# H3 mixer and token MLP on one core: half of W1's first block loaded early, and x normed behind the last evacuations

## The chip, the core and the metric

The kernel runs on one core of a Trainium2 chip. The metric is the device time of one execution in microseconds; the median of three runs of the kernel before is 181.79 us (181.39 to 182.12). A profiled execution gives the trace that the prediction reads.

## The reference

All arrays are bfloat16, S = 2048 positions by D = 448 channels, F = 1792 hidden units. The first half is an H3 mixer: a four-tap shift convolution of k, a product with v, a causal long convolution over S by FFT, a gate with the normed x. The second half is an MLP over the token axis.

```
k_shift = sum_t k[s - 3 + t] * shift_k[:, 3 - t]
kv = k_shift * v
y  = irfft(rfft(kv padded to 2S) * rfft(ssm_k padded to 2S))[:S] + kv * ssm_D
h  = x + layernorm(x) * y                       # x = A_q
n  = layernorm(layernorm(h))
u  = gelu(einsum("sd,sf->df", n, w1) + b1)      # contraction over the S tokens
h2 = h + (einsum("df,fs->ds", u, w2) + b2).T
```

## The kernel before

The 2048 positions are held as 128 partitions by R = 16 rows, so that an activation is 16 tiles of 128 x 448. One large SBUF array ("arena") holds everything; its regions are reused by offset. TensorE writes into PSUM ("ps"), which has 8 banks of 128 x 448 f32.

The stages, in the order in which they are written:

- loads: SP issues the loads of k (KH), v (V), the filter (KN) and small vectors (L866 to L886).
- kv: TensorE transposes k (L936, reads KH), convolves with diagonal matrices (L955), DVE multiplies with v (L961).
- kT, k1, k2 and u1, u2: the FFT of the filter and of kv in two matmul stages (L1015, L1050), with evacuations on ACT or DVE (L717 to L721, L1025) and a shuffle across partitions by DMA between the stages (L1031, on POOL's and SP's queues).
- i1: DVE forms the complex products (L1083), TensorE the first inverse stage (L1095), the results are evacuated into TU (L717, L720), and DMAs shuffle them into TZ: L1119 for the first seven pairs of rows, L1108 for the last pair, split over the queues of POOL, SP and ACT.
- q and xn: statistics of x by row (bn_stats L1155, bn_aggr L1157, then POOL L1160 and L1163 for the reciprocal root); for the first NX = 4 rows x is also normed into XN (L1185 on ACT or L1187 on DVE), which lies over TK.
- warm: filler matmuls (L1129) while the last shuffle is under way.
- i2: for each row r two matmuls (L1215) read TZ row r, a gate on ACT or DVE (L1224, L1226) and a combination on DVE (L1234, or L1244 for the first four rows) make h in f32; sums and squares (L1262, or L1250 for rows 0 and 1), a short chain on POOL (L1272 to L1286) and a DVE normalization (L1293) make Q row r, the MLP's input.
- mlp: the first seven 128-wide chunks of F accumulate row by row in seven PSUM banks (L1340, weights W1A); the other seven run chunk by chunk (L1350, weights W1B), each with a gelu (L1330); then the second layer by output row (L1362, weights W2), a final add on DVE (L1365) and stores.

The weights come by emit_w1_load and emit_w2_load on SP: four loads for W1A (L1313), four for W1B (L1317), four for W2 (L1324). W1A row group h occupies the arena from byte 7168 h per partition; KH is bytes 0 to 14335, KT 17024 to 31359, so that the first two groups lie over KH and the other two over KT. All of them depend on shuf["zpool"], the last large shuffle DMA.

The instruction order is made by a small list planner in the file (class _Sched). Each step of a stage, a step being a new pair of stage name and time mark, takes its due time from the table WHEN, in the order in which the steps are emitted. Among the operations whose predecessors are done in the planner's model, each engine takes the one with the lowest due time. An operation that may run on ACT or DVE (FX) takes a letter from WHERE: a for ACT, d for DVE, f for either. A semaphore wait is emitted only for real dependencies (`preds`); the `safter` edges order the plan and nothing else.

Of the kernel before, what the change touches and what calls it, by code (L numbers as in the profile page):

```python
# [9 lines left out]

ENGS = ("pe", "act", "dve", "pool", "sp")
WHEN = {
    "dummy": (69,),
    "tables": (172, 222, 238, 115, 211, 90, 258, 324,),
    "loads": (189, 214, 205, 290, 237, 82, 264, 277, 251, 276, 104, 283, 244, 317, 322,),
    "kv": (253, 110, 128, 123, 135, 121, 85, 66, 113, 159, 149, 191, 230, 266, 235, 142, 275,),
    "kT": (114, 112, 155, 152, 96, 80, 177, 176,),
    "k1": (188, 194, 229, 249, 190, 192, 213, 216, 218, 221, 227, 241, 185, 255, 269, 284,),
    "k2": (93, 139, 239, 168, 180, 225, 273, 295, 321, 320, 313, 314, 262, 293, 318, 315,),
    "u1": (250, 270, 274, 304, 287, 299, 311, 316, 268, 271, 296, 298, 301, 303, 306, 307,),  # L20
    "xload": (291, 182, 300, 223,),
    "ct": (100,),
    "bias": (178,),
    "q": (248, 233, 76, 233, 234, 329, 330, 332, 333,),
    "u2": (89, 97, 118, 141, 132, 137, 117, 91, 199, 164, 246, 219, 145, 156, 278, 281,),
    "i1": (151, 43, 55, 45, 52, 46, 58, 51, 74, 67, 64, 61, 150, 88, 56, 54,),
    "xn": (215, 265, 285, 232, 207, 256,),
    "w1a": (208, 148, 107, 323,),
    "w1b": (130,),
    "warm": (184, 183, 158, 65, 62, 83, 57, 125, 126, 127, 63, 59, 86, 209, 210, 187, 179, 106, 129, 167, 161, 157,  # L30
        153, 206, 193, 181, 196, 120, 101, 72, 32, 0, 47, 169,),
    "i2": (170, 1, 327, 10, 15, 6, 138, 4, 49, 9, 14, 3, 7, 243, 11, 2, 13, 17, 242, 25, 108, 103, 111, 282, 40, 163,
        220, 197, 12, 31, 257, 247, 286, 35, 60, 99, 312, 160, 140, 254, 308, 44, 41, 68, 22, 20, 98, 133, 245, 261,
        38, 29, 204, 289, 162, 18, 26, 240, 305, 294, 202, 154, 102, 263, 259, 201, 309, 39, 302, 328, 16, 147, 71,
        200, 326, 325, 27, 42, 30, 174, 94, 297, 75, 267, 195, 203, 331, 36, 272, 186, 260, 136, 92, 165, 24, 116,
        292, 217, 53, 231, 95, 70, 124, 105, 23, 48,),
    "w2": (198,),
    "mlp": (280, 166, 171, 212, 50, 28, 134, 122, 119, 226, 37, 112, 81, 21, 19, 5, 87, 144, 34, 84, 33, 131, 79, 8,
        146, 78, 77, 175, 224, 310, 109, 236, 228, 279, 143, 173, 252, 73, 288, 319,),
}  # L40
WHERE = {
    "kv": "affdfaaf",
# [5 lines left out]
    "bias": "d",  # L48
    "u2": "dfaafdaafaffafaa",
    "i1": "aaaafaaaaaafdaff",  # L50
    "xn": "afdf",
    "i2": "fffadaaaaffd",
}


# [515 lines left out]
def _build(nc, A_q, A_k, A_v, A_shift_k, A_ssm_k, A_ssm_D, B_w1, B_b1, B_w2, B_b2, out):  # L571
# [5 lines left out]
    Bsz, S, D = A_q.shape  # L577
# [22 lines left out]
    o_TK = 31360  # L600
# [25 lines left out]
    with ctx:  # L626
        sch = _Sched(nc, ctx, n_dma_sems=112, small_off=SMALL)
# [26 lines left out]
        TU = view(o_TU, [R, 2, D])  # L654
# [40 lines left out]
        def Ppair(b):  # L695
            s0, s1 = b.slots
            return PS[:, s0:s1 + 1, 0:D]
# [342 lines left out]
        shuf = {}  # L1040
# [28 lines left out]
                     est={"act": 904.0, "dve": 600.0})  # L1069

        i1_last = []

        def emit_products_i1():
            for jj in range(R // 2):
                ms = []
                for h in range(2):
                    i = 2 * jj + h
                    sch.t0 = T_I1 + T_DI1 * i
                    m = _Buf(mring)
                    ms.append(m)  # L1080
                    ru = (o_TU + i * 2 * DB, 2 * DB)
                    aft = [x for w in wbufs for x in w.readers] if i == 0 else [mfirst[0]]
                    op("dve", lambda e, W, m=m, i=i: e.tensor_tensor(  # L1083
                        out=MR(m.slots[0]).rearrange("p (x y) d -> p x y d", x=2),
                        in0=TU[:, i].unsqueeze(2).broadcast_to([128, 2, 2, D]),
                        in1=TK[:, i].unsqueeze(1).broadcast_to([128, 2, 2, D]), op=ALU.mult),
                       r=[ru, (o_TK + i * 2 * DB, 2 * DB)], bw=[m], n=4 * D, after=aft)
                    if i == 0:
                        mfirst.append(len(sch.ops) - 1)
                bs = [_Buf(psum, 2) for _ in range(2)]  # L1090
                for h in range(2):
                    for t, (tab, xy) in enumerate(((MA, 0), (MN, 3), (MB, 1), (MB, 2))):
                        for par in range(2):
                            P = slice(64 * par, 64 * par + 64)
                            k = op("pe", lambda e, W, b=bs[h], m=ms[h], par=par, t=t, tab=tab, xy=xy, P=P: e.matmul(  # L1095
                                Pb(b, par), tab[P, :], MR(m.slots[0])[P, xy, :], start=(t == 0), stop=(t == 3)),
                               r=r_iv, br=[ms[h]], bw=[bs[h]], n=D, est=94.5, mode=3)
                            i1_last.append(k)
                    evac(lambda jj=jj, h=h: TU[:, 2 * jj:2 * jj + 2, h, :], lambda b=bs[h]: Ppair(b),
                         [(o_TU + (4 * jj + h) * DB, DB), (o_TU + (4 * jj + 2 + h) * DB, DB)], bs[h], 2 * D)  # L1100
                if jj == R // 2 - 1:
                    for h in range(2):
                        for par in range(2):
                            j = 2 * jj + par
                            p0 = 64 * (j & 1) + 32 * ((j >> 1) & 1) + (j >> 2)
                            o_h = o_TU + (2 * j + h) * DB
                            for q_, a, b_, j0 in (("sp" if h and par else "pool", 0, 112, 0), ("act" if h else "sp", 112, 128, 14)):
                                k = op(q_, lambda e, W, j=j, h=h, p0=p0, a=a, b_=b_, j0=j0: e.dma_start(  # L1108
                                    TZ[p0:p0 + 29:4, j0:j0 + (b_ - a) // 8, h, :], TU[a:b_, j, h, :]),
                                       r=[(o_h, DB)], w=[(o_TZ + j0 * 2 * DB, (b_ - a) // 8 * 2 * DB, "zpool" if a == 0 else "zsp")],  # L1110
                                       dmab=(b_ - a) * DB, keng=8)
                                if a == 0:
                                    shuf["zpool"] = k
                    continue
                for par in range(2):
                    j = 2 * jj + par
                    p0 = 64 * (j & 1) + 32 * ((j >> 1) & 1) + (j >> 2)
                    for q_, a, b_, j0 in (("pool", 0, 112, 0), ("sp", 112, 128, 14)):
                        shuf["z" + q_ + str(j)] = shuf["z" + q_] = op(q_, lambda e, W, j=j, p0=p0, a=a, b_=b_, j0=j0: e.dma_start(  # L1119
                            TZ[p0:p0 + 29:4, j0:j0 + (b_ - a) // 8].rearrange("p r c d -> p r (c d)"),  # L1120
                            TU[a:b_, j].rearrange("p c d -> p (c d)")),
                           r=[(o_TU + j * 2 * DB, 2 * DB)], w=[(o_TZ + j0 * 2 * DB, (b_ - a) // 8 * 2 * DB, "z" + q_)],
                           dmab=(b_ - a) * 2 * DB, keng=8)
# [43 lines left out]
        def emit_xn():  # L1167
            for g in range(NX // 2):
# [5 lines left out]
                   est=290.0, r=rs, w=[(x, 4) for x, _ in rw])  # L1174
# [4 lines left out]
                for i in range(2):  # L1179
                    r = 2 * g + i  # L1180
                    sch.t0 = T_Q + 0.5 + T_DQ * g + 0.1 * (i + 1)

                    def norm(e, W, r=r):
                        if W == "act":
                            return e.activation(out=XN[:, r, :], in_=X[:, r, :], func=ACT.Identity, bias=qx[:, r, 1:2],  # L1185
                                                scale=qs[:, r, 3:4])
                        return e.tensor_scalar(out=XN[:, r, :], in0=X[:, r, :], scalar1=qs[:, r, 0:1],  # L1187
                                               scalar2=qs[:, r, 3:4], op0=ALU.subtract, op1=ALU.mult)
                    op(FX, norm, r=[(o_X + r * DB, DB), (o_qst + 16 * r, 16), (o_qx + 8 * r, 8)],
                       w=[(o_TK + r * 4 * D, 4 * D)], n=D, est={"act": 590.0, "dve": 430.0})  # L1190

        GR = ((0, 1), (1, 1)) + tuple((2 + 2 * g, 2) for g in range(7))
        o_hst = small(10 * 64)
# [114 lines left out]
        def emit_w1_load(which):  # L1308
            for h in range(4):
                sch.t0 = (T_W1 - 30.0 * (h > 1), T_WB - 30.0)[which] + 0.1 * h * (1 - which)  # L1310
                rs = slice(4 * h, 4 * h + 4)
                if which == 0:
                    wl[0] = op(WQ, lambda e, W, rs=rs: e.dma_start(W1A[:, rs, :], w1d[:, rs, 0:896]),  # L1313
                       w=[(o_W1A + 4 * h * 1792, 4 * 1792)], dmab=128 * 4 * 1792,
                       after=[shuf["zpool"]], safter=(wl[0],) if h else ())
                else:
                    wl[0] = op(WQ, lambda e, W, rs=rs: e.dma_start(W1B[:, rs, :], w1d[:, rs, 896:1792]),  # L1317
                       w=[(o_W1B + 4 * h * 1792, 4 * 1792)], dmab=128 * 4 * 1792, after=[shuf["zpool"]], safter=(wl[0],))
# [106 lines left out]
```

## Time and profile before

| | us |
|---|---|
| median of three runs | 181.79 |
| profiled execution | 182.27 |
| its span, first to last instruction | 180.20 |
| PE busy | 170.7 |
| DVE busy | 104.8 |
| ACT busy | 91.2 |
| POOL busy | 63.2 |

The granted TensorE clock was 1.00 throughout. Busy time of PE is no measure of need, since filler matmuls count in it; the stages have different limits, so the profile is read by stage. A group's line gives the number of instructions, the busy time, and the idle time ahead of them with what ended it. The chain of waits follows the work that ended last back to the start.

### The profile page before, as it was taken

How to read it: one execution, taken by the hardware profiler on the slowest of the kernel's cores; microseconds unless marked ns; L12 is line 12 of the kernel's file. 1: busy time of each engine (PE TensorE's matmuls, PEld its weight loads, DVE VectorE, ACT ScalarE, POOL GpSimd, SP SyncE). 2: the span in 40 equal slices, each digit the busy share in tenths (PEclk: the TensorE clock that was granted, in tenths of full speed). 3: DMA queues.
4: the chain of work that ended last, by engine and by line, in shares of the span. 5: the costliest groups of instructions: out<-in, count | busy, mean ns of one | idle time of the engine just before them, and what ended most of it. 6: DMA issues, size and time to landing. Idle time of an engine off the chain costs nothing.

```text
span 180.2 us, 3395 instructions
## 1 busy us (share of the span) xinstructions
PE 170.7 (95%) x1333; PEld 97.5 (54%) x1333; DVE 104.8 (58%) x182; ACT 91.2 (51%) x129; POOL 63.2 (35%) x157
## 2 busy tenths in 40 slices
PE   6999999999889999898898999999999999999994
PEld 2888746543223332244343545556565677777784
DVE  7998677669889999999998645000000053322331
ACT  3897375689899999953985264710221100000000
POOL 8641209562950148797389953000000000000000
DMA  5997008686784947663999999990000001111122
GB/s 178 389 409 251 5 4 308 225 312 186 262 266 131 365 126 210 201 206 89 375 378 401 405 417 421 417 415 28 4 0 0 0 0 40 66 51 51 51 76 76
DMA packets 15347, 35.11 MB, mean 195 GB/s; under 512 B 3724, under 2 KB 9388, under 8 KB 15332
## 3 DMA queue, kind: packets, MB, share of 16 engines
q1 hardware_dynamic: 12068, 28.00, 41.8%
q0 software_dynamic: 3072, 6.80, 11.9%
q8 instruction: 10, 0.16, 0.4%
q10 hardware_dynamic: 192, 0.11, 0.2%
q14 instruction: 5, 0.04, 0.1%
HBM read 22.05 MB, written 1.84 MB: 133 GB/s over the span
## 4 chain that ended last, share of the span: by engine, by line
PE 65%; DVE 12%; ACT 10%; DMA 5%; POOL 3%; issue 2%; SPq 1%; DVEq 0%; POOLq 0%
PE ps L1362 23%; PE ps L1350 12%; PE ps L1340 9%; PE ps L955 7%; DVE arena L1083 5%; DMA arena<-arena 5%; PE ps L1015 4%; ACT arena L1025 4%; ACT arena L717 2%; PE ps L994 2%; PE ps L1050 2%; ACT arena L718 2%; PE ps L1095 1%; POOL arena L1286 1%; ACT arena L826 1%
## 5 line engine op out<-in xcount | busy, mean ns | idle before, releaser
L1362 PE MATMUL ps<-arena 128*128 128x448 bf16 (+2 forms) x238 | 43.5, 342 | 0.0
L1365 DVE SCALAR_TENSOR_TENSOR arena<-ps,arena 128x448 bf16<-128x448 f32 (+2 forms) x17 | 11.1, 656 | 54.2 <-PE ps L1362 54.2
L1362 PEld LDWEIGHTS ps<-arena 128*128 128x128 bf16 x238 | 32.9, 145 | 10.1 <-ACT arena L1330 0.8
L1340 PE MATMUL ps<-arena 128*128 128x448 bf16 x112 | 23.4, 353 | 0.6 <-DVE arena L1293 0.6
L1031 POOL DMA_DIRECT2D arena<-arena x32 | 17.5, 553 | 17.3 <-ACT arena L1025 16.3
L717 ACT CAST arena<-ps 128x896 bf16<-128x896 f32 x28 | 23.3, 979 | 0.4
L1350 PE MATMUL ps<-arena 128*128 128x448 bf16 x112 | 22.8, 352 | 0.0
L1025 ACT CAST arena<-ps 128x896 bf16<-128x896 f32 x22 | 18.9, 913 | 6.6 <-PE ps L1015 5.7
L1330 ACT ACTIVATE arena<-ps,arena 128x448 bf16<-128x448 f32 x14 | 8.3, 638 | 22.4 <-PE ps L1350 18.7
L1050 PE MATMUL ps<-arena 128*64 128x448 bf16 x128 | 16.0, 361 | 1.1 <-ACT arena L1025 0.7
L1340 PEld LDWEIGHTS ps<-arena 128*128 128x128 bf16 x112 | 10.6, 98 | 11.5 <-DVE arena L1293 2.2
L1083 DVE TENSOR_TENSOR arena<-arena 128x1792 bf16<-128x1792 bf16 x16 | 16.6, 1083 | 0.1
L1350 PEld LDWEIGHTS ps<-arena 128*128 128x128 bf16 x112 | 10.9, 98 | 10.1 <-DVE arena L1226 0.3
L1095 PE MATMUL ps<-arena 64*128 64x448 bf16 x128 | 14.1, 351 | 1.7 <-ACT arena L717 1.0
L1015 PE MATMUL ps<-arena 128*32 128x448 bf16 x256 | 14.8, 355 | 0.5 <-ACT arena L718 0.3
L955 PE MATMUL ps<-arena 112*128 112x224 bf16 (+3 forms) x112 | 13.4, 273 | 0.0
L1119 POOL DMA_DIRECT2D arena<-arena x14 | 8.3, 595 | 12.7 <-ACT arena L717 12.3
L955 PEld LDWEIGHTS ps<-arena 112*128 112x128 bf16 x112 | 9.2, 98 | 4.4 <-DVE arena L1025 0.9
L1050 PEld LDWEIGHTS ps<-arena 128*64 128x64 f16 x128 | 5.3, 108 | 11.4 <-ACT arena L717 3.7
L1262 ACT ACTIVATE arena<-arena 128x448 bf16<-128x448 f32 x14 | 8.1, 576 | 6.1 <-DVE arena L1234 6.0
L961 DVE TENSOR_TENSOR arena<-ps,arena 128x896 bf16<-128x896 f32 x8 | 8.6, 1089 | 4.3 <-PE ps L955 4.2
L1095 PEld LDWEIGHTS ps<-arena 64*128 64x128 f16 x128 | 5.0, 94 | 10.7 <-ACT arena L717 6.0
(93 smaller groups left out, 209.6 us busy)
## 6 DMA issues: line engine op xcount, KB each, us to landing
arena<-in_B_w_dram SPq DMA_DIRECT2D x8, 896.0 KB, 12.1
arena<-in_B_w_dram SPq DMA_DIRECT2D x2, 2048.0 KB, 17.0
arena<-arena SPq DMA_DIRECT2D x16, 224.0 KB, 3.2
arena<-arena POOLq DMA_DIRECT2D x32, 112.0 KB, 3.4
arena<-in_B_w_dram SPq DMA_DIRECT2D x2, 1536.0 KB, 19.5
arena<-arena POOLq DMA_DIRECT2D x14, 196.0 KB, 4.2
arena<-in_A_k_dram SPq DMA_DIRECT2D x4, 448.0 KB, 6.0
arena<-in_A_v_dram SPq DMA_DIRECT2D x4, 448.0 KB, 9.9
```

Of the source, the lines that this page charges most:

```text
L717: return e.copy(out=dst(), in_=src())
L955: op("pe", lambda e, W, b=b, i=i, cc=cc, dl=dl, i0=i0, i1=i1, rs=rs, sh=sh: e.matmul(Pb(b, i)[:, 112 * i0:112 * i1 + 112], KX[cc][0:112, i ...
L1015: op("pe", lambda e, W, b=b, r=r, q=q, x=x, c0=c0: e.matmul(PS[32 * q:32 * q + 32, b.slots[x], 0:D], E[:, 2 * r + x, c0:c0 + 32], src[:, r ...
L1025: return e.copy(out=dst, in_=Ppair(b)) if W == "act" else e.tensor_copy(out=dst, in_=Ppair(b))
L1031: shuf[tag].append(op(q_, lambda e, W, g=g, i=i, a=a, nu=nu, jh=jh: e.dma_start(T[a + i:a + i + 4 * nu - 3:4].rearrange("p (j k) c d -> p ...
L1050: op("pe", lambda e, W, b=bs[h], h=h, j=j, c=c, par=par: e.matmul(PS[64 * par:64 * par + 64, b.slots[c], 0:D], FW[:, 64 * c:64 * c + 64], ...
L1083: op("dve", lambda e, W, m=m, i=i: e.tensor_tensor(out=MR(m.slots[0]).rearrange("p (x y) d -> p x y d", x=2), in0=TU[:, i].unsqueeze(2).br ...
L1095: k = op("pe", lambda e, W, b=bs[h], m=ms[h], par=par, t=t, tab=tab, xy=xy, P=P: e.matmul(Pb(b, par), tab[P, :], MR(m.slots[0])[P, xy, :], ...
L1340: op("pe", lambda e, W, r=r, fc=fc, b=bs[fc]: e.matmul(Pb(b), W1A[:, r, 128 * fc:128 * fc + 128], Q[:, r, :], start=(r == 0), stop=(r == R ...
L1350: op("pe", lambda e, W, r=r, fc=fc, b=b: e.matmul(Pb(b), W1B[:, r, 128 * (fc - n0):128 * (fc - n0) + 128], Q[:, r, :], start=(r == 0), sto ...
L1362: op("pe", lambda e, W, r=r, fc=fc, b=b, d0=d0, d1=d1: e.matmul(Pb(b)[:, d0:d1], W2[fc // 7][:, fc % 7, r:S:R], G[:, fc, d0:d1], start=(fc ...
L1365: op("dve", lambda e, W, r=r, b=b, A=A, d0=d0, d1=d1: e.scalar_tensor_tensor(out=X[:, r, d0:d1], in0=Pb(b)[:, d0:d1], scalar=bm[:, r:r + 1 ...
```

## The change

Three edits are made.

1. In emit_w1_load the first two groups of W1A no longer depend on shuf["zpool"]; what is left is that KH must have been read. The other two keep the dependency.
2. The norms of x for the first four rows get a `safter` edge on the last evacuation of i1.
3. The due times in WHEN are given as decimals. Sorted by due time, all entries outside q, xn, warm, i2 and mlp stand in the same order as before; those five have other values. The letters of xn and i2 in WHERE change.

```diff
-    "w1a": (208, 148, 107, 323,),
+    "w1a": (2654.22, 2601.22, 2565.22, 2779.22,),
...
-    "q": (248, 233, 76, 233, 234, 329, 330, 332, 333,),
+    "q": (2686.67, 2692.38, 2558.85, 2728.33, 2726.2, 2724.82, 2729.2, 2733.43, 2725.05,),
...
-    "xn": (215, 265, 285, 232, 207, 256,),
+    "xn": (2725.33, 2727.89, 2403.48, 2719.09, 2605.55, 2614.65,),
...
-    "i2": (170, 1, 327, 10, 15, 6, 138, 4, 49, 9, 14, 3, 7, 243, 11, 2, 13, 17, 242, 25, 108, 103, 111, 282, 40, 163,
+    "i2": (2602.37, 0, 2723.32, 764.4, 756.9, 1409.88, 2536.4, 934.78, 1089.89, 765.9, 756.4, 1486.7, 1497, 2662.27,
...
-    "xn": "afdf",
-    "i2": "fffadaaaaffd",
+    "xn": "addf",
+    "i2": "aaffafaaddff",
...
         i1_last = []
+        evl = []
...
-                    evac(lambda jj=jj, h=h: TU[:, 2 * jj:2 * jj + 2, h, :], lambda b=bs[h]: Ppair(b),
+                    ke = evac(lambda jj=jj, h=h: TU[:, 2 * jj:2 * jj + 2, h, :], lambda b=bs[h]: Ppair(b),
                          [(o_TU + (4 * jj + h) * DB, DB), (o_TU + (4 * jj + 2 + h) * DB, DB)], bs[h], 2 * D)
                 if jj == R // 2 - 1:
+                    evl.append(ke)
...
                     op(FX, norm, r=[(o_X + r * DB, DB), (o_qst + 16 * r, 16), (o_qx + 8 * r, 8)],
-                       w=[(o_TK + r * 4 * D, 4 * D)], n=D, est={"act": 590.0, "dve": 430.0})
+                       w=[(o_TK + r * 4 * D, 4 * D)], n=D, est={"act": 590.0, "dve": 430.0}, safter=evl)
...
             for h in range(4):
                 sch.t0 = (T_W1 - 30.0 * (h > 1), T_WB - 30.0)[which] + 0.1 * h * (1 - which)
+                if which == 0 and h < 2:
+                    sch.t0 = -5.0 + h
                 rs = slice(4 * h, 4 * h + 4)
                 if which == 0:
                     wl[0] = op(WQ, lambda e, W, rs=rs: e.dma_start(W1A[:, rs, :], w1d[:, rs, 0:896]),
                        w=[(o_W1A + 4 * h * 1792, 4 * 1792)], dmab=128 * 4 * 1792,
-                       after=[shuf["zpool"]], safter=(wl[0],) if h else ())
+                       after=[shuf["zpool"]] if h > 1 else (), safter=(wl[0],) if h else ())
```

## The prediction, made before the change was run

> **What bounds the kernel now.** I read the chain of waits first, to see which stretches set the end, then busy time by stage, then each engine in order of time around the seam at 77 to 97 us. Of the chain:
>
> ```profile
> 78.28 0.67 SPq L1108
> ...
> 79.00 4.93 DMA arena<-arena
> ...
> 83.97 0.57 PE ps L1215 x2
> ...
> 96.10 0.57 DVE arena L1293
> ...
> 96.71 6.85 PE ps L1340 x35
> ...
> 141.84 35.47 PE ps L1362 x196
> ```
>
> The columns are start, length and what ran. A block transfer bridges 79.00 to 83.93; a chain of small work runs from there to 96.71; from 96.71 to 177.32 every piece is TensorE. The view by stage:
>
> ```profile
> 77.20:83.97 6.77, 6.22 (x32) 3.04 (x33) 6.38 (x22) 2.79 (x4) 6.15 (x14) 1.00 0.61 175
> 83.97:89.56 5.59, 4.91 (x25) 2.37 (x26) 5.24 (x16) 4.21 (x8) 1.87 (x5) 1.00 0.79 269
> 89.56:96.71 7.15, 6.57 (x34) 2.96 (x33) 6.09 (x19) 5.68 (x16) 6.57 (x15) 1.00 1.05 387
> 96.71:108.40 11.69, 11.69 (x62) 5.75 (x63) 7.82 (x23) 5.41 (x13) 8.64 (x21) 1.00 1.04 410
> ```
>
> Columns: window, length, busy us (instructions) of PE, weight loads, DVE, ACT, POOL, then clock, DMA share, GB/s. PE's 6.22 us in the first row is filler (L1129). From 96.71 on PE runs 62 matmuls in 11.69 us, 0.189 us each, without a hole. So the kernel is a front part up to 96.71, an 80.6 us PE block that only fewer matmuls would shorten, and a 2.9 us tail. The question is whether the change brings 96.71 forward.
>
> The timelines of the engines at the seam:
>
> ```profile
> 76.14 1.39 SPq L1119 DMA_DIRECT2D arena<-arena  x2
> 77.57 2.11 SPq L1108 DMA_DIRECT2D arena<-arena  x3
> ```
> ```profile
> 77.02 0.76 ACT L1185 ACTIVATE arena<-arena 128x448 f32<-128x448 bf16 x1
> 77.68 0.89 ACT L717 CAST arena<-ps 128x896 bf16<-128x896 f32 x1
> 78.61 1.98 ACTq L1108 DMA_DIRECT2D arena<-arena  x2
> ```
> ```profile
> 78.75 0.24 POOL L1160 TENSOR_SCALAR arena<-arena 128x2 f32<-128x2 f32 x1
> 79.06 0.63 POOL L1108 DMA_DIRECT2D arena<-arena  x1
> ```
>
> The reader sees a norm of x (L1185) in front of the last evacuation (L717), whose input, the last L1095 matmul, is done at 77.09. The reader should also see that SP issues without a break from 76.14 to 79.68.
>
> **What the skill says.** "DMA: Bandwidth & Descriptors", section "Issuing engines are not separate DMA queues": transfers of all issuing engines share the same 16 engines, so an early load is free only where these are idle. The trace agrees: they are 0.02 busy in 18 to 27 us (last fence below) and 1.04 busy in the third and fourth rows above. "Anatomy of one DMA" on the same page gives about 2 us fixed per transfer; the seam's 98 KB pieces take 4.3 to 5.0 us from issue to landing, so the trace's number is used. "Perfetto Trace Analysis", section "Identifying the Most-Contended Engine", warns that matmul busy time misleads; I count matmuls at 0.189 us instead.
>
> **Part 1, half of W1A early.** Rows 0 to 7 of W1A lie over KH, last read by the transposes L936 (last at 15.3 us). SP has nothing to issue between 9.4 and 26.40 us, so both loads go out at about 15.5, at 0.4 to 0.7 us each (L1313's issues). Nothing queues behind their wait but the first shuffles at 26.40.
>
> ```profile
> 18.00:27.00 9.00, 8.98 (x118) 5.43 (x116) 6.08 (x9) 4.84 (x6) 1.56 (x4) 1.00 0.02 4
> ```
>
> They carry 2 x 917.5 KB; at the 410 GB/s of the fourth row above that is 4.5 us, behind the input loads that drain at about 18. Landing: about 23, 3 us before the first shuffle. Cost 0; upper bound 0.5 us if late inputs (the small bias loads, on which L914 waits until 19.8) are disturbed. POOL's queue issues nothing there until 26.69.
>
> At the other end L1313 issues two loads instead of four after 83.94, and everything behind moves 4.5 us forward. Does anyone wait for it? No wait at L1340 or L1350 names a weight DMA. The first L1340 (89.56) starts after Q of L1293 (88.82 + 0.48 = 89.30), while its weights landed at 83.94 + 4.7 = 88.6. W1B's last load lands at 93.7 + 13.2 = 106.9, before its first use at 108.36. All weight waits are covered before and better covered after. Value: 0 in the old order. It opens up to 0.7 us only if Q comes earlier than 88.6, the point from which W1A would be next in line.
>
> **Part 2, norms behind the last evacuation.** The extra edge orders the planner's list only; no semaphore is added. It takes L1185 (0.76 us) from in front of L717, which can then start at about 77.15 instead of 77.68: 0.53 us. Where does that go? POOL's last L1108 waits for this evacuation and could issue at 78.75 instead of 79.06: 0.3 us. But SP's third L1108 carries the other part of the same data, and SP is busy issuing until 78.95; the evacuation was over at 78.57 already. So SP's train is next in line, and nothing in the change shortens it. The reading L1215 needs every piece. Bounds 0 to 0.5 us of gain; I take 0.1.
>
> The norms themselves (ACT 0.76, DVE 0.56) move behind 77.2. Engines before: three on ACT, one on DVE; after, the letters "addf" put two on DVE, one on ACT, one free. ACT is idle from 82.17 to 85.32, so its share is hidden. DVE gains 0.5 us inside 77.20 to 83.97, where it is 6.38 of 6.77 busy with the statistics L1155 (12 rows by 84.2 at about 0.6 us with their L1157). So about one row of statistics slides behind 83.97.
>
> **Part 3, the order of the second half.** Sorted by due time, all entries outside q, xn, warm, i2 and mlp stand as before, so the plan up to about 67 us should be the old one. Those five are shuffled: agreement in rank between old and new i2 entries is only about 0.3. On PE the second-layer inputs I2 still begin with row 0; the front groups of rows 0 and 1 stay near the front on DVE; the six pairs of statistics after the first two stand together in the middle (places 255 to 272 of 335) where two were first and four last. Gates fixed to DVE change from rows 8 and 15 to 12 and 13.
>
> What can be won: in 83.97 to 96.71 (12.74 us) PE runs 26 L1215, 28 L1340 and 4 fillers, 58 x 0.189 = 10.9 us, so 1.8 us of holes and 0.75 of fillers: at most 2.5. What can be lost: DVE is idle 0.35 + 1.06 = 1.4 us in the same stretch; added work there beyond that delays Q. Added at most: the displaced row 0.6, the last pair of statistics that now runs at 97.78 (1.35 with its aggregates), and up to two more gates of 0.65 drawn in: 3.2, so a loss of at most 1.8. The old trace does not show the new order. Nothing in it says which way; I take 0, with -2.5 and +1.8 kept for the range.
>
> **Sum.** 0 + (-0.1) + 0 = -0.1 us. The profiled execution took 182.27 us with a span of 180.20, so 2.07 lie outside the span; it stands 0.48 above the median 181.79. The sum is a difference of spans: profiled 182.2, median 181.7.
>
> **The cases.** About 0.9 us (0.5%) is what a measurement here can tell from no change.
>
> 1. Forecast: L1215 starts within 0.3 us of 83.97 and the fill takes as long as before, 181.7; own range 180.9 to 182.6. For: SP's unbroken train, covered weights, a PE-bound block. Against: an entirely new order. Chance 0.43.
>
> 2. Faster: the new order, with W1A's first half resident, feeds PE without holes, so half of the 2.5 us goes: 181.7 - 1.2 = 180.5, at the utmost 179.2. For: L1340 waits 2.2 us on L1293 in this stretch, and L1215 1.1 us on ACT's gates; that is order, not work. Against: the rstd path POOL L1272 to L1286 (1.03 + 0.5 + 0.5 and more) stays. Chance 0.25.
>
> 3. Slower: DVE takes over in 83.97 to 96.71. Its 1.4 us of slack take the second norm and one displaced row of statistics (1.1); from there on the pair drawn from 97.78 and gates on DVE stand in front of Q. With 2.7 us added, L1293's Q are 1.3 late and so is PE's gapless block: 183.1, at the utmost 183.6. For: the norms go to DVE, statistics leave last place, DVE is 11.33 of 12.74 busy. Against: DVE has 3.9 us idle in the next window. Chance 0.28.
>
> 4. The change doesn't do what it says: the early loads are planned late or the free evacuation goes to DVE behind statistics, and all stays at 181.8. Chance 0.04.
>
> **Numbers.** Predicted 181.7. The range 180.3 to 183.2 takes in most of cases 2 and 3; the likeliest one's own range is 180.9 to 182.6. Faster by over 0.5% (below 180.9): case 2 but for a little, 0.25. Slower (above 182.7): case 3, 0.29 with the edge of case 1. Same: 0.46.
>
> **What would show it.** Right: two L1313 issues at 15 to 17 us and an idle DMA slice filled; first shuffle still at 26.4; last L717 ending near 78.05; SP's last L1108 still near 79.0 and the first L1215 near 83.9; PE gapless from 96 to 97. Case 2: gapless before 95.8. Case 3: after 97.6, with L1340 waiting for L1293 behind L1155 on DVE. I would be wrong in kind if the early loads push the first L1031, if SP's train begins earlier than 76.1, or if a hole opens in the block after 97.

## The result, and the profile after

The changed kernel takes 185.19 us (median of four runs, 184.48 to 185.5) where the kernel before took 181.95 beside it (four runs): ratio 1.0181, 95% interval 1.0162 to 1.02. It is slower by 3.2 us, outside the predicted range. Its profiled execution took 185.5 us with a span of 183.3, against 182.27 and 180.20.

In kernel.py of the changed kernel the lines lie 14 to 18 further down: the products with v are L975, the bias cast L928, the first shuffle L1045, the second inverse stage L1231, its gate L1240 (ACT) or L1242 (DVE), statistics of x L1171, L1173, L1176, L1179, sums of a pair on POOL L1288, L1291, L1293, L1298, the reciprocal root L1302, Q L1309, the first layer L1358 and L1368, the second L1380. I call the stretch that begins with the first L1215 (L1231) the fill: in it the 16 rows of Q are made and the first layer starts.

The chain of waits of the changed kernel, in order of time (start, length, what ran):

```profile
8.73 11.75 DMA arena<-in_B_b_dram
...
20.51 0.04 DVE arena L928
...
20.59 1.10 DVE arena L975
...
84.43 0.93 PE ps L1231 x4
...
89.25 0.98 POOL arena L1302
...
100.59 0.72 POOL arena L1179
...
101.30 0.66 POOL arena L1302
...
103.00 0.68 POOL arena L1179
...
103.70 0.70 DVE arena L1242
...
104.45 0.55 PE ps L1231 x2
...
144.02 36.42 PE ps L1380 x201
```

Two things are new in it. At the front stands the small load of b2 and the bias cast L928 behind it. And in the fill the chain stays on POOL from 89.25 until 103.68, goes by a gate on DVE, and gives way to TensorE only at 104.45; before it was TensorE's from 96.71 on.

The view by stage, same windows and columns as in the prediction:

```profile
77.20:83.97 6.77, 6.68 (x39) 3.18 (x35) 6.54 (x23) 2.82 (x4) 6.65 (x15) 1.00 0.64 179
83.97:89.56 5.59, 4.73 (x25) 2.17 (x23) 5.36 (x18) 3.39 (x7) 2.58 (x7) 1.00 0.74 243
89.56:96.71 7.15, 5.95 (x21) 2.40 (x22) 6.54 (x21) 6.23 (x17) 6.40 (x13) 0.76 1.05 399
96.71:108.40 11.69, 11.18 (x60) 5.43 (x58) 8.04 (x22) 4.42 (x12) 9.38 (x24) 1.00 1.03 417
```

In the third row PE ran 21 matmuls where it ran 34 before. The timelines of SP and of DVE (start, length, instruction, idle time ahead of it with its releaser):

```profile
15.61 0.95 SPq L1331 DMA_DIRECT2D arena<-in_B_w_dram  x2
27.12 26.69 SPq L1045 DMA_DIRECT2D arena<-arena  x16
...
78.07 2.19 SPq L1124 DMA_DIRECT2D arena<-arena  x3
```
```profile
20.51 0.17 DVE L928 CAST arena<-arena 128x16 f32<-128x16 bf16 x1 [2.15 <-DMA arena<-in_B_b_dram]
20.59 2.08 DVE L975 TENSOR_TENSOR arena<-ps,arena 128x896 bf16<-128x896 f32 x2
...
84.03 1.12 DVE L1171 BATCH_NORM_STATS2 arena<-arena 128x6 f32<-128x448 bf16 x2
85.38 1.28 DVE L1260 SCALAR_TENSOR_TENSOR arena<-ps,arena 128x448 f32<-128x448 f32 x2 [0.23 <-PE ps L1231]
```

The early loads are issued where the prediction had them, at 15.61. The first shuffle comes at 27.12 instead of 26.40, and the fill begins at 84.43 instead of 83.97. The span grew by 3.1 us: 0.46 of it lies ahead of the fill, and 2.64 from the fill's start to the end (183.3 - 84.43 = 98.87 against 180.20 - 83.97 = 96.23). Two statistics of x (L1171) run from 84.03 to 85.15, across the start of the fill; before, the last one there ended at 84.21, 0.24 us after its start:

```profile
83.62 0.59 DVE L1155 BATCH_NORM_STATS2 arena<-arena 128x6 f32<-128x448 bf16 x1
```

### The profile page after: what moved, and what is told of

Same layout as the page of the kernel before. It is cut to its first block, busy times and chain, and to the rows that moved or that the text cites. A ratio compares the mean times of both kernels' runs of the same rounds, so it can differ in the third digit from the quotient of the medians.

```text
span 183.3 us, 3392 instructions
## 1 busy us (share of the span) xinstructions
PE 172.9 (94%) x1333; PEld 98.2 (54%) x1333; DVE 105.3 (57%) x183; ACT 90.6 (49%) x128; POOL 62.9 (34%) x157
## 4 chain that ended last, share of the span: by engine, by line
PE 60%; ACT 13%; POOL 7%; DMA 6%; DVE 6%; SPq 4%; issue 2%; DVEq 0%; POOLq 0%
PE ps L1380 23%; PE ps L1368 12%; DMA arena<-in_B_b_dram 6%; PE ps L1358 6%; ACT arena L731 6%; PE ps L1029 5%; ACT arena L1039 5%; PE ps L969 5%; PE ps L1145 4%; ACT arena L732 3%; PE ps L1064 3%; PE ps L1110 2%; POOL arena L1302 2%; DVE arena L1098 2%; DVE arena L1260 1%
## 5 line engine op out<-in xcount | busy, mean ns | idle before, releaser
L1380 PE MATMUL ps<-arena 128*128 128x448 bf16 (+2 forms) x238 | 44.0, 342 | 0.0
L1380 PEld LDWEIGHTS ps<-arena 128*128 128x128 bf16 x238 | 32.7, 145 | 10.7 <-ACT arena L1348 1.9
L1358 PE MATMUL ps<-arena 128*128 128x448 bf16 x112 | 25.0, 367 | 0.7 <-DVE arena L1309 0.7
L1045 POOL DMA_DIRECT2D arena<-arena x32 | 17.5, 553 | 17.8 <-ACT arena L1039 16.8
L1368 PE MATMUL ps<-arena 128*128 128x448 bf16 x112 | 22.7, 352 | 0.0
L1348 ACT ACTIVATE arena<-ps,arena 128x448 bf16<-128x448 f32 x14 | 8.9, 633 | 24.5 <-PE ps L1368 19.8
L1358 PEld LDWEIGHTS ps<-arena 128*128 128x128 bf16 x112 | 11.2, 102 | 12.1 <-issue 1.8
L1368 PEld LDWEIGHTS ps<-arena 128*128 128x128 bf16 x112 | 10.9, 98 | 10.1 <-ACT arena L1348 0.7
L1064 PEld LDWEIGHTS ps<-arena 128*64 128x64 f16 x128 | 5.3, 108 | 11.3 <-ACT arena L731 3.7
L975 DVE TENSOR_TENSOR arena<-ps,arena 128x896 bf16<-128x896 f32 x8 | 8.6, 1090 | 4.3 <-PE ps L969 4.2
```

The lines of the kernel that those rows point to most:

```text
L1045: shuf[tag].append(op(q_, lambda e, W, g=g, i=i, a=a, nu=nu, jh=jh: e.dma_start(T[a + i:a + i + 4 * nu - 3:4].rearrange("p (j k) c d -> p ...
L1064: op("pe", lambda e, W, b=bs[h], h=h, j=j, c=c, par=par: e.matmul(PS[64 * par:64 * par + 64, b.slots[c], 0:D], FW[:, 64 * c:64 * c + 64], ...
L1358: op("pe", lambda e, W, r=r, fc=fc, b=bs[fc]: e.matmul(Pb(b), W1A[:, r, 128 * fc:128 * fc + 128], Q[:, r, :], start=(r == 0), stop=(r == R ...
L1368: op("pe", lambda e, W, r=r, fc=fc, b=b: e.matmul(Pb(b), W1B[:, r, 128 * (fc - n0):128 * (fc - n0) + 128], Q[:, r, :], start=(r == 0), sto ...
L1380: op("pe", lambda e, W, r=r, fc=fc, b=b, d0=d0, d1=d1: e.matmul(Pb(b)[:, d0:d1], W2[fc // 7][:, fc % 7, r:S:R], G[:, fc, d0:d1], start=(fc ...
```

## The experiments

Each kernel was timed beside the kernel before on the same chip, and the ratio is to that. In the first four the kernel before took 181.77 us. Diffs are cut to the lines that matter.

**Which of the three edits.** Four kernels take them apart: the early load alone; the changed kernel with its first half of W1A behind the shuffle again; early load and edge with the old table; the edge alone (its list of the last evacuations, evl, is filled as in the change).

```diff
  early load alone (on the kernel before)
-                       after=[shuf["zpool"]], safter=(wl[0],) if h else ())
+                       after=[shuf["zpool"]] if h > 1 else (), safter=(wl[0],) if h else ())
  new table without early load (on the changed kernel)
-                       after=[shuf["zpool"]] if h > 1 else (), safter=(wl[0],) if h else ())
+                       after=[shuf["zpool"]], safter=(wl[0],) if h else ())
  edge alone (on the kernel before)
-                       w=[(o_TK + r * 4 * D, 4 * D)], n=D, est={"act": 590.0, "dve": 430.0})
+                       w=[(o_TK + r * 4 * D, 4 * D)], n=D, est={"act": 590.0, "dve": 430.0}, safter=evl)
```

> The kernel before with the early load of two W1A groups alone; old due times, no edge. Theory A (two separate losses: the early load delays the small bias load, behind which DVE's multiplications with v queue, and the new order starves the fill): the bias cast starts 0.5 to 0.8 us later than before (20.3 to 20.6 us), the first L1215 is 0.4 to 0.5 later (84.4), time 182.3 to 182.6. Rival B (the early load carries the whole loss through the DMA queues): about 185. Rival C (the early load is free and the 0.7 us of the trace is scatter): 181.9, cast at 19.8.

> The changed kernel with all four W1A loads behind the last shuffle again; new due times and edge stay. Theory A: the front is back to the old times (first L1231 at 83.9 to 84.0), the fill is as starved as in the changed kernel, time 184.5 to 184.8. Rival B: 181.9. Rival C: 185.2.

> The changed kernel with the old due times and letters; early load and edge stay. Theory A: the early load's 0.4 to 0.5 us minus at most 0.3 from the edge: 182.0 to 182.5, and a gapless PE block from about 97. Rival B: about 185. Rival C: 181.6 to 181.9.

> The kernel before with the planner's edge alone. If SP's row of issues sets the last shuffle, as predicted, the last evacuation ends 0.5 us earlier, the first L1215 stays within 0.3 us of 83.97 and the time at 181.6 to 181.9. If the evacuation sets it, the first L1215 comes 0.5 us earlier and the time is 181.3 to 181.5.

| kernel | us | ratio, interval | cast starts | first shuffle | fill starts | span |
|---|---|---|---|---|---|---|
| before (profile) | | | 19.79 | 26.40 | 83.97 | 180.2 |
| early load alone | 182.45 | 1.0034 (1.0021 to 1.0048) | 21.09 | 27.70 | 84.59 | 181.0 |
| new table, no early load | 184.23 | 1.0142 (1.012 to 1.0163) | 19.66 | 26.27 | 83.25 | 182.0 |
| early load and edge, old table | 182.75 | 1.0063 (1.004 to 1.0087) | 20.36 | 26.97 | 84.41 | 180.6 |
| edge alone | 182.04 | 1.0014 (1.0004 to 1.0023) | 19.29 | 26.15 | 83.10 | 179.6 |
| changed kernel | 185.19 | 1.0181 (1.0162 to 1.02) | 20.51 | 27.12 | 84.43 | 183.3 |

The early load costs 0.34%, the edge gains nothing, and the new table carries 1.42%. Early load and new table make 1.76%, the changed kernel's 1.81% within the intervals. Under the new table the edge changes no instruction's place, so that the kernel without the early load is also the new table by itself. The times came within 0.3 us of what was expected for two separate losses. One expectation failed in kind: if SP's issues set the last shuffle, the two kernels with the edge and without the early load were to start the fill at about 83.97; they started it at 83.25 and 83.10, without being faster for it. Part 2 below comes back to this.

The timeline of DVE, in the kernel before and then with the early load alone, shows what the 0.34% are:

```profile
19.79 0.17 DVE L914 CAST arena<-arena 128x16 f32<-128x16 bf16 x1 [1.46 <-DMA arena<-in_B_b_dram]
```
```profile
21.09 0.17 DVE L914 CAST arena<-arena 128x16 f32<-128x16 bf16 x1 [2.75 <-DMA arena<-in_B_b_dram]
21.18 2.08 DVE L961 TENSOR_TENSOR arena<-ps,arena 128x896 bf16<-128x896 f32 x2
```

DVE waits 2.75 us for b2 (1.46 before), and the products with v, which the first shuffle needs, stand behind the cast in its queue. In the three traces of the table with the early load the cast starts at 20.36 to 21.09, in the three without at 19.29 to 19.79; the first shuffle follows by 6.6 to 6.9 us in all six. (Of the 1.30 us between the two lines above, 0.41 come from a later issue of b2's load, at 9.46 against 9.05, which the edit doesn't explain.) The view by stage, of the kernel before and then of the changed one, shows where the early load falls:

```profile
9.00:18.00 9.00, 9.00 (x117) 7.71 (x116) 8.18 (x13) 8.06 (x9) 2.69 (x7) 1.00 0.90 331
```
```profile
9.00:18.00 9.00, 9.00 (x117) 7.73 (x116) 8.12 (x13) 8.06 (x9) 2.63 (x7) 1.00 1.01 355
```

The DMA engines (last but one column) are 0.90 busy from 9.00 to 18.00 in the kernel before, and the early load is issued at 15.6, into that.

**Does it go by the cast?** If the late b2 costs only because DVE waits for it, putting the cast on POOL frees the products with v, and the early load should be cheap again.

```diff
-            op("dve", lambda e, W: e.tensor_copy(out=b2c, in_=b2n), r=[(o_b2n, 32)], w=[(o_b2c, 64)], n=16)
+            op("pool", lambda e, W: e.tensor_copy(out=b2c, in_=b2n), r=[(o_b2n, 32)], w=[(o_b2c, 64)], n=16)
```

> The kernel before with the bias cast L914 on POOL instead of DVE. Theory A (the cast's wait for the small bias load holds up DVE's in-order queue): L961 no longer waits 1 to 1.5 us behind the cast, the first shuffle L1031 goes out 0.3 to 0.8 us before 26.4, time 181.0 to 181.5. Rival (the front is set by TensorE or by the late filter load, the cast's wait is covered): first shuffle at 26.2 to 26.5, time 181.7 to 181.9. The planner moves some instructions of DVE for it, so 0.2 either way is no evidence.

> The same with the early load of two W1A groups added. Theory A: the bias load still lands late (about 20.4 to 21.1), but only POOL waits for it, so the time is that of the kernel with the cast on POOL within 0.3 us. Rival B2 (the early load delays other input loads or the shuffles): 0.5 to 0.8 us above that kernel, as the early load costs with the cast on DVE.

The cast on POOL alone took 181.52 us (0.9986, 0.9977 to 0.9994), with the early load 181.57 (0.9996, 0.9983 to 1.001), beside 181.80 before. The early load's cost falls from 0.34% to 0.10% by the ratios, within their intervals nothing. The timelines of POOL and DVE with the early load and the cast on POOL:

```profile
20.17 0.20 POOL L914 CAST arena<-arena 128x16 f32<-128x16 bf16 x1 [2.27 <-DMA arena<-in_B_b_dram]
```
```profile
18.76 1.09 DVE L961 TENSOR_TENSOR arena<-ps,arena 128x896 bf16<-128x896 f32 x1 [0.44 <-PE ps L955]
20.43 1.09 DVE L961 TENSOR_TENSOR arena<-ps,arena 128x896 bf16<-128x896 f32 x1 [0.57 <-PE ps L955]
```

b2 is still late, but only POOL waits for it. The products wait for TensorE alone, and the first shuffle is issued at 26.16. So the path is shown: late b2, cast, DVE's queue, shuffle. The cast was not the only bound, though: the shuffle was expected 0.3 to 0.8 us before 26.4 with the cast on POOL, and without the early load it stood at 26.47. In no trace of this case does it come before 26.15, so another bound lies there; which one wasn't tried. The edge of part 2 added to the cast on POOL brought nothing:

> The kernel before with the edge of part 2 and the bias cast L914 on POOL instead of DVE, old table, no early loads. The cast on POOL alone gave 181.52 us (0.9986) and the edge alone 1.0014. If the edge is neutral to harmful as measured: 181.5 to 181.9 us (0.9986 to 1.0005). If the edge's loss came only from a chance fit of the seam: under 181.4.

It took 181.54 us (0.999, 0.9979 to 1.0002). The three can't be told from each other. The cast on POOL by itself, with 0.9986, is the version here that computes the whole reference and is quicker than the kernel before, by a little.

**What limits the fill?** Theory P: POOL's chain, L1272 to L1286 for each pair of rows, which the chain of waits follows. Theory D: DVE, the prediction's case 3. A reciprocal root that is cheap tells them apart: in these two kernels the power on POOL is a multiplication, so that the reciprocal root is left out of the computation.

```diff
-                                                                                 op=ALU.pow),
+                                                                                 op=ALU.mult),
```

> The changed kernel without the early load, with POOL's power in the fill's chain (L1302) turned into a multiplication: the reciprocal root of h's second norm is left out, the plan stays the same. Theory P (under the new order POOL's chain of small operations starves TensorE of Q): the power shrinks from 0.7 to 1.1 us to about 0.2, the loss of 2.6 us against the old order falls to less than 1, time 181.5 to 182.7. Rival D (the order on DVE, or of TensorE's own queue, is what starves it): 183.5 to 184.2.

> The kernel before with the same power turned into a multiplication, the reciprocal root left out. Its holes in the fill add up to 1.8 us, of which Q takes about 1.2: theory P 180.8 to 181.5, with TensorE's block gapless from 0.3 to 1 us earlier. Rival D: 181.6 to 181.9.

Under the new table (without the early load) it took 182.61 us, 1.0063 (1.0039 to 1.0087), 1.6 us less than with the power; under the old one 180.81, 0.9949 (0.9933 to 0.9966), 1.0 us less. On POOL the pair's root falls from 958 to 402 ns in the old order (mean of six, between 84 and 108 us):

```profile
L1286 POOL TENSOR_TENSOR arena<-arena 128x2 f32<-128x2 f32 x6 | 5.7, 958 | 0.2
```
```profile
L1286 POOL TENSOR_TENSOR arena<-arena 128x2 f32<-128x2 f32 x6 | 2.4, 402 | 0.2
```

So POOL's chain bounds the fill in both; whether more in the new, the intervals don't tell. But with it shortened 1.8 us are left between the two tables: P alone isn't the loss. PE's timeline under the new table with the cheap root shows what is left:

```profile
89.23 0.55 PE L1231 MATMUL ps<-arena 128*128 128x448 bf16 x2 [1.15 <-ACT arena L1240]
90.52 0.55 PE L1358 MATMUL ps<-arena 128*128 128x448 bf16 x2 [0.74 <-DVE arena L1309]
```

These two stops near the start of the fill stay as long as with the power, 1.89 us together against a single one of 0.68 in the old order with the cheap root. The later stops, which the section on the prediction lists, are gone. So the late stops go by POOL's chain, and the early ones don't.

**Which part of the new table.** Of the due times of q, xn, warm, i2 and mlp, those of TensorE's own steps were put in the new relative order alone, then all the others with the new letters, then the letters alone. The planner makes a new plan from any such edit, so the parts aren't perfectly apart.

```diff
  letters alone
-    "xn": "afdf",
-    "i2": "fffadaaaaffd",
+    "xn": "addf",
+    "i2": "aaffafaaddff",
```

> The kernel before with only the due times of TensorE's own steps (L1215, L1340 and the fillers L1129) taken in the new relative order; all other due times and the letters are old. Theory M (the matmul order itself costs: only two instead of six L1340 stand behind row 0's Q, and L1215 of a row whose bank is freed late stands in front of the rest): ratio 1.008 to 1.016, 183.2 to 184.7 us, PE's first L1340 at about +6.9 us after the first L1215. Theory V (gates, combinations and POOL's chain come in an order that frees banks and finishes Q late, whatever PE's order): ratio within 0.4% of 1, under 182.5 us.

> The kernel before with the due times of all steps of q, xn and i2 that are not TensorE's in the new relative order, and the new letters; TensorE's own steps keep their old ones. Theory M: ratio within 0.4% of 1. Theory V: ratio 1.008 to 1.016, 183.2 to 184.7 us, POOL again with L1176 and L1179 ahead of L1286 for rows 10 and 11. If both this and the run with TensorE's order alone cost under 0.4%, the loss is in how the two fit together.

> The kernel before with the new letters of xn and i2 alone (which norms and gates go to ACT and which to DVE); all due times are old. If the fixed gates (eight of twelve letters a, f or d differ) are what frees the banks late: ratio 1.006 to 1.014, with L1215 or the first L1340 waiting for an ACT gate. If the order is, and not the choice of engine: ratio within 0.4% of 1, at most 182.5 us.

TensorE's order alone took 182.9 us (1.0056, 1.0038 to 1.0074), the rest 183.34 (1.0073, 1.0045 to 1.01). Neither theory's range was met: each part costs something, and the two make 1.29%, near the 1.42% of the whole table. The letters alone took 184.37 (1.013, 1.0103 to 1.0156). This looked like the whole loss, although the same letters together with the new due times of these steps had cost only 0.73%. With them ACT does the gate of row 8, which DVE did at 86.97 before, and PE stood still for a gate on ACT:

```profile
90.30 0.55 PE L1215 MATMUL ps<-arena 128*128 128x448 bf16 x2 [1.61 <-ACT arena L1224]
```

Theory G says that this one gate makes the loss, Theory S that no single letter does. Four kernels tested that:

```diff
  row 8 on ACT (on the kernel before)
-    "i2": "fffadaaaaffd",
+    "i2": "fffaaaaaaffd",
  row 8 on DVE (on the letters alone, and on the changed kernel without early load)
-    "i2": "aaffafaaddff",
+    "i2": "aaffdfaaddff",
  all old letters (on the changed kernel without early load): as in the kernel before
```

> The kernel before with one letter changed: the gate of row 8 goes to ACT (d to a); due times old. Theory G (this one gate, the sixth on ACT before a bank comes free, makes the loss): ratio 1.008 to 1.014, PE idle 1.2 to 1.8 us for L1224 on ACT ahead of the second batch of L1215, first Q of L1293 at about +7 us after the first L1215. Theory S (no single letter matters; the old due times and letters fit each other and any change of either costs something): 1.003 to 1.007, as for PE's order alone.

> The kernel before with all the new letters but row 8's, which stays on DVE. Theory G: within 0.4% of 1, where all the new letters gave 1.013. Theory S: 1.005 to 1.012, a part of the loss only.

> The changed kernel with its early load left out, and row 8's gate on DVE. Theory G: 1.000 to 1.005 instead of 1.0142, with PE gapless from about 12.7 us after the first L1215. Theory S: at least 1.008, since the new due times stay.

> The changed kernel with its early load left out and all the old letters: the new due times alone. If the letters carry the loss: 1.000 to 1.004. If the due times cost by themselves what PE's and the others' new order cost (0.56% and 0.73% with letters): 1.006 to 1.013. Above 1.013 the new letters would even have helped the new due times.

| kernel | us | ratio, interval |
|---|---|---|
| row 8 on ACT, old table | 183.55 | 1.01 (1.0064 to 1.0136) |
| new letters but row 8 on DVE, old due times | 182.91 | 1.0053 (1.003 to 1.0076) |
| new table, row 8 on DVE, no early load | 184.78 | 1.017 (1.0126 to 1.0215) |
| new due times, all old letters, no early load | 184.81 | 1.0165 (1.0131 to 1.02) |

For the changed kernel Theory G falls: with the new due times neither row 8 on DVE nor all the old letters help. In the old table the letter costs 1.0%, as much as Theory G expected, but not by its mechanism: in that trace PE's longest stops in the fill are 0.69 and 1.00 us, both for DVE. PE's timeline in the kernel of the last row, the new due times alone:

```profile
90.83 1.82 PE L1358 MATMUL ps<-arena 128*128 128x448 bf16 x7 [3.53 <-DVE arena L1309]
```

One stop of 3.53 us for the first Q that it can use, where the kernel before had stops of 0.68 and 0.58. So the new due times make a loss of this size by themselves, with each of the three sets of letters tried.

**Two more kernels.** The due times of q and xn alone (statistics and norms of x), and the other half of theory P, POOL relieved by giving a pair's four small operations to DVE (with the bias cast on POOL):

```diff
-                    op("pool", lambda e, W, hs=hs: e.tensor_scalar(out=hs[:, 4:6], in0=hs[:, 0:2], scalar1=1.0 / D,
+                    op("dve", lambda e, W, hs=hs: e.tensor_scalar(out=hs[:, 4:6], in0=hs[:, 0:2], scalar1=1.0 / D,
...
-                op("dve" if ng == 1 else "pool", lambda e, W, var=var: e.tensor_scalar(
+                op("dve", lambda e, W, var=var: e.tensor_scalar(
```

> The kernel before with the due times of q and xn alone (statistics of x and norms of x) in their new relative order, letters old. If the statistics of x, moved ahead of the rows' own chain on POOL, hold most of the 0.73%: ratio 1.005 to 1.010, and the eleventh and twelfth Q at +20.4 us or later after the first L1215 instead of +19.5. If i2's own due times hold it: within 0.3% of 1.

> The kernel before with the bias cast L914 on POOL and, for the pairs of rows, L1272, L1275, L1277 and L1282 on DVE, so that POOL keeps only the pow L1286 of each pair; due times and letters old. Theory P (POOL's chain limits the fill): about as good as the short pow, ratio 0.992 to 0.997, 180.4 to 181.2 us. If DVE becomes the bound instead (28 more small operations, at about 0.1 us each 2.8 us more in a stretch where it has 1.4 us idle): 1.002 to 1.010.

The order of q and xn alone took 183.06 us, 1.0071 (1.0057 to 1.0085), the size expected. The place was another than I wrote: the eleventh and twelfth Q came at +19.8 and +20.2 after the start of the fill, hardly later than before (+19.5 and +20.0), the first at +6.4 instead of +5.3. The timeline of DVE (its line numbers are six lower than before's):

```profile
83.28 1.14 DVE L1149 BATCH_NORM_STATS2 arena<-arena 128x6 f32<-128x448 bf16 x2
...
84.42 0.60 DVE L1149 BATCH_NORM_STATS2 arena<-arena 128x6 f32<-128x448 bf16 x1
85.14 0.68 DVE L1238 SCALAR_TENSOR_TENSOR arena<-ps,arena 128x448 f32<-128x448 f32 x1
```

The last statistic ends at 85.02, 0.85 us after the start of the fill at 84.17; before it ended 0.24 after. The first combination waits behind it, PE's fillers in the fill are eight instead of four, and the first Qs follow later. In these two profiled executions that is 0.5 us from the start of the fill to the end (96.73 against 96.23), while the medians differ by 1.3; where the rest lies isn't shown.

With the small operations on DVE the time was 185.76 us, 1.0226 (1.0201 to 1.0251): the opposite of what theory P hoped for. The view by stage and PE's timeline of that kernel:

```profile
89.56:96.71 7.15, 4.25 (x24) 2.00 (x22) 7.07 (x33) 6.33 (x18) 1.72 (x3) 1.00 1.06 388
```
```profile
95.53 2.63 PE L1340 MATMUL ps<-arena 128*128 128x448 bf16 x13 [2.90 <-DVE arena L1293]
```

POOL is busy 1.72 us there instead of 6.57, but DVE 7.07 of 7.15, each small operation at 154 to 160 ns where 0.1 us was expected, and PE waits 2.90 us for one Q. So DVE can't take this work of POOL; the other way was not tried. Not all of the 2.3% is this wait: two executions at full TensorE clock took 184.32 and 184.96 us, 1.4% and 1.8% over the kernel before, and four with a mean clock of about 0.99 took 185.42 to 186.47.

## Why the prediction was wrong

**The step that failed most is Part 3**: "Nothing in it says which way; I take 0." The new order costs 1.42% without the early load, about 2.5 us. In that kernel's own profile it is 98.75 us from the start of the fill to the end (182.0 - 83.25), 2.52 more than before. PE's timeline shows where, at full clock throughout, first in the kernel before and then with the new order:

```profile
89.36 0.55 PE L1215 MATMUL ps<-arena 128*128 128x448 bf16 x2 [0.68 <-ACT arena L1224]
...
96.71 6.85 PE L1340 MATMUL ps<-arena 128*128 128x448 bf16 x35 [0.58 <-DVE arena L1293]
```

```profile
88.90 0.55 PE L1231 MATMUL ps<-arena 128*128 128x448 bf16 x2 [1.14 <-ACT arena L1240]
90.12 0.54 PE L1358 MATMUL ps<-arena 128*128 128x448 bf16 x2 [0.67 <-DVE arena L1309]
...
93.15 0.55 PE L1358 MATMUL ps<-arena 128*128 128x448 bf16 x2 [0.39 <-DVE arena L1309]
...
99.35 3.22 PE L1358 MATMUL ps<-arena 128*128 128x448 bf16 x15 [0.46 <-DVE arena L1309]
103.11 0.55 PE L1231 MATMUL ps<-arena 128*128 128x448 bf16 x2 [0.54 <-DVE arena L1242]
```

The stops make 3.20 us where the kernel before had 0.68 + 0.58 = 1.26. They lie in three places: the gate on ACT and the Q ahead of the first L1358 (6.87 us after the start of the fill, 5.78 before), two Qs (at 93.15 and 99.35) that POOL's chain releases late, and a gate on DVE at 102.37 that waited 0.60 us for POOL's L1179:

```profile
102.37 0.68 DVE L1242 TENSOR_SCALAR arena<-ps,arena 128x448 f32<-128x448 f32 x1 [0.60 <-POOL arena L1179]
```

The view by stage over 24 us from the start of the fill, before and with the new order:

```profile
83.97:107.97 24.00, 22.74 (x117) 10.94 (x118) 18.73 (x55) 15.09 (x35) 17.00 (x39) 1.00 0.99 370
```
```profile
83.25:107.25 24.00, 20.74 (x104) 9.24 (x104) 19.72 (x57) 14.12 (x35) 18.35 (x41) 1.00 1.00 374
```

PE ran 104 matmuls, its few fillers included, instead of 117; 13 x 0.189 = 2.5 us, the whole difference. (By busy time, and by the stops, it is 2.0 and 1.9 us; the rest is in pauses too short to be listed or in the records.)

As to the parts: TensorE's own new order alone brings 0.56%, the new places of x's statistics and norms alone 0.71%. They sum to 1.27%, close to the table's 1.42%. That their sum is the explanation isn't shown: each part was planned anew, and other parts don't add at all. The new letters cost 1.30% alone and 0.73% with their due times, and the single letter that cost 1.0% in the old order brought nothing in the new one.

The bound of Part 3, +1.8 us, was too small as well. It counted work added to DVE against DVE's slack of 1.4 us. But in the first 12.70 us of the fill DVE was busy 12.05 us with the new order and 11.29 before, only 0.76 more, and the new order still cost 2.5 us:

```profile
83.25:95.95 12.70, 10.47 (x53) 4.74 (x53) 12.05 (x37) 9.93 (x23) 9.36 (x19) 1.00 0.95 340
```

The bound left out that POOL is as full as DVE (6.57 of 7.15 us in the row that the prediction shows) and works in a fixed order, so that a gate or a Q waits for whatever stands ahead of it there, and that a changed order of matmuls costs without any engine getting much more work.

**Case 3** named the right sign, and part of the mechanism: statistics of x were displaced across the start of the fill, as the timeline of DVE after shows (84.03 to 85.15, against an end at 84.21 before). The price of case 3, 183.1 and at the utmost 183.6, fell short of 184.23 for the order by itself. Its sentence that DVE takes over is half right at most: the chain of waits in the changed kernel runs over POOL until 103.68, and a cheap root on POOL takes 1.6 us off.

**Part 1** took 0 and named the right cause in its bound, "0.5 us if late inputs (the small bias loads, on which L914 waits until 19.8) are disturbed". That is what happened, at 0.34% or 0.6 us, a little over the bound. The step that failed was the choice of 0. I read the DMA engines as idle from the window 18 to 27, while the loads go out at 15.6, when they were 0.90 busy. "DMA: Bandwidth & Descriptors", section "Issuing engines are not separate DMA queues", says that all transfers interleave on the same engines, which agrees with b2's delay here; the prediction cited it and then looked at the wrong window. The other end held: the weights' earlier arrival gave nothing, since with the cast on POOL, where the early load disturbs nothing, it is no gain either (181.57 against 181.52).

**Part 2** took a gain of 0.1 us, with bounds of 0 to 0.5, and the edge alone measured +0.14%, about 0.3 us slower. As a term of the sum it is small, but that it is near zero is luck, since its reason failed. Two kernels with the cast on POOL issue the first shuffle at the same 26.16, the one with the early load, which costs nothing measurable there, and the one with the edge. Their timelines of ACT's queue and of DVE, first without and then with the edge (line numbers two higher):

```profile
78.22 1.95 ACTq L1108 DMA_DIRECT2D arena<-arena  x2
...
84.08 1.27 DVE L1244 SCALAR_TENSOR_TENSOR arena<-ps,arena 128x448 f32<-128x448 f32 x2 [0.25 <-PE ps L1215]
```
```profile
77.77 1.98 ACTq L1110 DMA_DIRECT2D arena<-arena  x2
...
84.04 1.26 DVE L1246 SCALAR_TENSOR_TENSOR arena<-ps,arena 128x448 f32<-128x448 f32 x2
```

SP's three issues begin at 77.19 and 77.24, yet the fill begins at 83.49 without the edge and at 83.20 with it. So SP's train was not the next in line, as Part 2 says; the pieces on ACT's queue, which it left out, go out 0.45 us earlier with the edge. The gain then ends at DVE: without the edge its first combination waits for PE, with it the combination comes behind a statistic of x and starts no earlier. Under the new table the edge moves nothing.

**The cases.** Case 2 (the new order feeds PE without holes) is refuted by the stops above. Its argument also took the waits of the weight loads, 2.2 us on Q and 1.1 us on ACT's gates, for what PE could win; PE itself stood 0.58 and 0.68 us. Case 4 (early loads late, nothing changes) is refuted by their issue at 15.61 and by the time. Of the signs of being wrong in kind that the prediction listed two came true: the first shuffle was pushed, and holes opened after 97, at 99.35 and 103.11 in the kernel without early load and at 104.45 in the changed one.

## What to carry to other kernels

When a change brings a whole new order for a stretch where two or more engines are nearly full (here DVE 6.09 and POOL 6.57 of 7.15 us), an unknown sign isn't a zero. In this kernel a loss was the likelier: each of nine edits of due times or letters, whole or in part, cost 0.5 to 1.7%. Whether that holds for other kernels isn't shown. Read the load of the DMA engines at the moment of issue and not at the time when the data is wanted, and ask what small load is still under way then and which in-order queue has an instruction waiting for it. Before moving work off the engine that the chain of waits names, check the next engine's idle time in the same window: 28 small operations of 0.16 us were enough to turn a hoped-for gain into a loss of about 2%.

## What the runs showed of the hardware that was not expected

- A load of 4 KB (b2) took 10.7 us to land in the kernel before, and 9.9 to 11.0 in all 16 traces without the early load; in the four with it 11.3 to 11.8. So large loads issued more than 6 us after it hold it up.
- By the profile, the same form of operation on 128 x 2 numbers takes from 0.19 to 0.72 us on POOL (L1291 in the changed kernel without the early load), and a pair's power 0.69 to 1.16. What sets the length wasn't tried.
- In the changed kernel's profiled execution TensorE's clock fell to 0.76 in 89.56 to 96.71, 0.50 from 92 to 94, behind PE's stops of 1.14 and 0.66 us. "TensorE: Matmul & The Clock Gate", Part 1, says that idle time brings the half clock. The trace agrees only in part: the same kernel without the early load has stops of 1.14 and 0.67 us there and kept 1.00, and of the two profiled kernels with a stop of 3.53 us one kept 1.00 (row 8 on DVE) and one shows 0.991 over the execution (old letters).
- What the dip costs differs. It isn't the cause of the loss: the new order loses its 2.5 us in a trace at full clock, and of the changed kernel's four executions two show 0.991 and took 185.5 and 185.05 us, two show 1.0 and took 185.34 and 184.48. But with the early load alone the three executions of 22 at 0.991 took 184.18 to 184.77, the others 181.76 to 182.99; and with the new due times and row 8 on DVE the five at 0.981 to 0.991 took 184.63 to 185.96, the one at 1.0 took 183.97, so that a part of that kernel's 1.7% may be the dip.
